# A float64 weight join with its intermediate word in PSUM, a fused state update, and a new opening list, in a one-core RWKV and mixture-of-experts kernel

## Chip, core and metric

The kernel runs on one core of a Trainium2 chip. The metric is the device time of one execution in microseconds. "Before" has three timed runs and one profiled execution.

## What is computed

The reference is a float32 RWKV attention, a bilinear feed-forward layer and a soft mixture of eight experts. Cut to what matters:

```python
for t in range(S):                       # B=4, H=8, S=768, D=48
    cur = einsum(u * k_t, v_t)
    y[:, :, t] = einsum(r_t, state + cur)
    state = w_t[..., None] * state + einsum(k_t, v_t)
x = y.transpose(0, 2, 1, 3).reshape(3072, 384)
x = ((x @ w1) * (x @ w2)) @ w3 @ w_out   # weights are float64: 384x1024, 384x1024, 1024x1024, 1024x384
P = exp(x @ w_gate - max);  8 rounds of row and column normalisation (Sinkhorn)
out = sum over e of P[:, e] * (relu(x @ e_w1[e]) @ e_w2[e])
```

The four weights of the feed-forward layer arrive as float64, two 32-bit words each. The chip makes float32 of them: the exponent and upper mantissa come from the high word, three more mantissa bits from the low word, the sign from the high word.

## The kernel before, in words

All engines run fixed instruction lists; there is no planner on the chip, and each engine and each DMA queue works strictly in the order in which the Python code issued its instructions. The order of the first 28 slices (a slice is a quarter of an attention unit of 128 tokens; there are 24 units) is written out by hand in the table `START`: each word names a step and its index. From slice 28 on (`S0`) a loop over slices issues the steps. After the 96 attention slices and the feed-forward blocks, the experts take the rest of the time with another schedule; the change does not touch that part.

Steps of the opening that matter here:

- `ld.j` (line 200) loads piece j of the float64 weights. There are 20 pieces: 4 of w_out ("o", 768 words per partition), 8 of w3 ("3", 1024 words) and 8 of w1 and w2 ("i", 768 words). Four raw buffers take turns.
- `c1.j` (lines 187 and 188) is two ScalarE operations over the whole piece: the high word scaled by 2^-112 into the result tile, and the low word turned in place into three bits.
- `c2.j` (lines 193 and 194) is two VectorE operations over the whole piece: shift the scaled word left by 3 and OR the three bits in, then OR in the sign. Every operand lies in SBUF.
- `w34.s.g` is TensorE's product of w3 and w_out, 8 rows s of 8 steps g, so that the layer's two last matrices become one; step g needs columns g*128 of the piece of w3 and part g of w_out. `ws` and `w34l` split the result into a high and a low part.
- `hi` (ScalarE) and `lo` (GpSimd) split w1 and w2 likewise. Then `pa.b.f` and `pb.b.f` (line `ab`) are the two products of token block b with column block f, `asb` copies pa out, `gs` (line 465, VectorE) multiplies, `gh` and `gl` split, and `po` multiplies by the joined matrix.
- Attention of unit n: `scanF`, `scanG`, `small`, `ks`, `rp`, `cc` on VectorE; `kx`, `rx`, `rk`, `ec` on GpSimd; `sc`, `trn`, `yt1`, `up`, `yt2` on TensorE; `Sn` (lines 375 and 376) on VectorE makes the new state in two half steps, each a product TSt of the old state with the decay, and the addition of `up` out of PSUM.

PSUM banks of the pool `ps` come from one tag `moe` with four buffers, used by w34, pa, pb, po and the logits.

Of the kernel before, what the change touches and what calls it, by code (L numbers as in the profile page):

```python
# [27 lines left out]
ks.0 L.w.2 c1.0 small.0 L.k.2 rp.0 kx.0 L.r.2 c2.0 rx.0 trn.0 c1.1 sc.0 ld.4 scanG.1 kn.0 c2.1 ks.1 ld.5 scanF.1
L.k.3 c1.2 rk.0 small.1 L.w.3 rp.1 c2.2 L.r.3 c1.3 rx.1 L.kn.2 L.rn.2 kx.1 cc.0 w34.0.0 ld.6 c2.3 ec.0 w34.0.1 c1.4
rk.1 scanG.2 ld.7 w34.0.2 w34.0.3 L.kn.3 L.rn.3 w34.0.4 c2.4 c1.5 w34.0.5 cp.0 w34.0.6 ld.8 c2.5 w34.0.7 yt1.0 ws.0  # L30
up.0 w34l.0 L.v.2 Sn.0 w34.1.0 ld.9 c1.6 w34.1.1 w34.1.2 cc.1 yt2.0 scanF.2 ec.1 w34.1.3 xraw.0 sc.1 c2.6 L.w.4 rk.2
w34.1.4 c1.7 trn.1 w34.1.5 w34.1.6 cp.1 ld.10 kn.1 w34.2.0 L.kn.4 L.rn.4 c2.7 yt1.1 w34.2.1 up.1 w34.1.7 L.v.3
small.2 ld.11 w34.3.0 c1.8 Sn.1 w34.2.2 w34.3.1 rp.2 w34.2.3 ws.1 ks.2 yt2.1 rx.2 L.r.4 c2.8 w34.2.4 L.k.4 xraw.1
w34.3.2 kx.2 w34.2.5 w34.3.3 w34l.1 w34.2.6 cc.2 ld.12 trn.2 scanF.3 ec.2 w34.3.4 kn.2 w34.2.7 scanG.3 sc.2 c1.9
rk.3 w34.3.5 small.3 w34.4.0 L.w.5 cp.2 w34.3.6 rp.3 ws.2 w34.4.1 L.kn.5 L.rn.5 c2.9 w34.3.7 rx.3 L.r.5 c1.12
w34.4.2 yt1.2 w34l.2 w34.4.3 ws.3 ks.3 up.2 ld.13 w34.4.4 c1.10 L.v.4 w34l.3 Sn.2 L.k.5 w34.5.0 kx.3 w34.4.5 w34.5.1
cc.3 yt2.2 c2.10 ec.3 w34.4.6 xraw.2 sc.3 rk.4 c1.13 w34.4.7 xd.2 trn.3 cp.3 ld.14 w34.5.2 c2.12 w34.6.0 ws.4 L.kn.6
L.rn.6 w34.5.3 c1.11 w34l.4 w34.6.1 w34.5.4 c2.13 ld.16 w34.6.2 w34.5.5 hi.0 w34.6.3 kn.3 lo.0 c2.11 w34.5.6 hi.1
w34.6.4 xh.0 yt1.3 lo.1 w34.6.5 c1.14 up.3 w34.6.6 L.v.5 scanF.4 ld.15 w34.7.0 w34.6.7 w34.7.1 ws.6 scanG.4 w34.5.7
w34l.6 w34.7.2 small.4 ws.5 L.w.6 c2.14 w34.7.3 w34l.5 w34.7.4 c1.15 w34.7.5 ks.4 ld.17 w34.7.6 xl.0 hi.2 kx.4 L.k.6  # L40
w34.7.7 ws.7 Sn.3 pa.0.0 lo.2 asb.0.0 pb.0.0 c2.15 w34l.7 c1.16 yt2.3 pa.0.1 rp.4 hi.3 c2.16 rx.4 L.r.6 xraw.3
pb.0.1 lo.3 gs.0.0 hi.4 ld.18 trn.4 cc.4 pa.0.2 gh.0.0 scanG.5 kn.4 ec.4 c1.17 sc.4 scanF.5 pb.0.2 lo.4 asb.0.1 cp.4
L.w.7 pa.0.3 small.5 c2.17 gl.0.0 c1.18 yt1.4 rk.5 up.4 gs.0.1 hi.5 ld.19 L.v.6 ks.5 pb.0.3 gh.0.1 asb.0.2 gl.0.1
c2.18 L.kn.7 L.rn.7 L.k.7 pa.0.4 lo.5 gs.0.2 hi.6 Sn.4 kx.5 pb.0.4 c1.19 rp.5 yt2.4 lo.6 asb.0.3 cc.5 L.r.7 gh.0.2
pa.0.5 gs.0.3 xraw.4 c2.19 ec.5 gh.0.3 pb.0.5 asb.0.4 gl.0.2 scanG.6 hi.7 trn.5 gl.0.3 pa.0.6 kn.5 gs.0.4 lo.7
gh.0.4 asb.0.5 gs.0.5 gl.0.4 gh.0.5 pb.0.6 asb.0.6 gl.0.5 gs.0.6 pa.0.7 rx.5 gh.0.6 gl.0.6 asb.0.7 pb.0.7 scanF.6
# [9 lines left out]
def tile_rwkv_moe_sinkhorn_moe(  # L56
# [155 lines left out]
    def c1(j):  # L212
        kind, i = CONV[j]
        if kind == "o":
            c = wo[:, 2 * i:2 * i + 2, :].rearrange("p a d -> p (a d)")
        elif kind == "3":
            c = tmp.tile([P, FF], F32, tag="w3c", bufs=3, name="w3c")
        else:
            c = tmp.tile([P, KD * FC], F32, tag="cv", bufs=2, name="cv")
        conv1(raws[j], FF, c)  # L220
        cvs[kind, i] = c

    def c2(j):
        conv2(raws.pop(j), cvs[CONV[j]])

# [995 lines left out]
```

## Time and profile before

| what | value |
|---|---|
| median of 3 runs | 1995.4 us (1994.36 to 1997.26) |
| the profiled execution, its own time | 1995.78 us |
| its span in the trace | 1993.5 us |
| TensorE busy over the span | 97% |
| VectorE, ScalarE, GpSimd busy over the span | 72%, 34%, 34% |
| mean granted clock of TensorE | 0.997 |

The span is the time from the first to the last instruction in the trace; 2.3 us of the execution's own time lie around it. A busy TensorE is not TensorE at its peak, because matmuls are pipelined and their ends are modelled; an idle TensorE, though, has a named releaser. The profile's page has one strip of 40 slices of the span for each engine: TensorE's first digits are 5 and 8 and all later ones are 9, VectorE's are 8 and 9. The stage in question is therefore the first 150 us.

### The profile page before, as it was taken

Reading aid. Unit: us, or ns where it says so; the run is one execution under the profiler, and the core shown is the slowest. Engines: PE = TensorE matmul, PEld = TensorE weight load, DVE = VectorE, ACT = ScalarE, POOL = GpSimd, SP = SyncE. Lnnn points to the kernel's source line nnn. Section 1 sums busy time; section 2 is a strip of 40 time slices with the busy share of each in tenths; the row PEclk is TensorE's granted clock in tenths of the full one; section 3 lists DMA queues with packets and bytes.
Section 4 is the critical chain, followed back from the end, with each engine's and each line's share of the span. In section 5 each row is a group of like instructions: output and inputs, shape, how many; then the busy total and the mean of one; then the engine's idle time right before and its main releaser. Section 6 shows DMA issues by size and latency. Waiting matters only on the chain.

```text
span 1993.5 us, 37983 instructions
## 1 busy us (share of the span) xinstructions
...
## 2 busy tenths in 40 slices
...
GB/s 365 178 104 102 112 145 114 132 93 179 238 187 182 188 195 170 193 177 200 172 203 187 178 201 177 203 170 201 181 184 184 188 187 185 191 193 167 179 192 121
DMA packets 90492, 353.75 MB, mean 177 GB/s; under 512 B 10384, under 2 KB 34256, under 8 KB 64592
## 3 DMA queue, kind: packets, MB, share of 16 engines
...
q14 instruction: 50, 0.41, 0.1%
...
## 4 chain that ended last, share of the span: by engine, by line
PE 87%; DVE 3%; DMA 1%; ACT 1%; issue 1%; POOL 0%; SPq 0%; DVEq 0%; ACTq 0%; POOLq 0%
PE yp L108 38%; PE zp L108 33%; PE po L108 5%; PE pa L108 4%; PE pb L108 4%; PE yt L108 1%; DMA xd<-x2s 1%; DVE ct L883 1%; DVE hl L880 1%; PE sc L108 1%; PE up L108 0%; PE trn L108 0%; DVE x2s L674 0%; PE pl L108 0%; POOL x2s L674 0%
## 5 line engine op out<-in xcount | busy, mean ns | idle before, releaser
L108 PE MATMUL zp<-xc,w1c 128*128 128x256 f32 x5760 | 841.8, 282 | 8.8 <-ACT ct L890 7.8
L108 PEld LDWEIGHTS zp<-xc,w1c 128*128 128x128 f32 x5760 | 790.3, 189 | 26.2 <-ACT ct L890 10.4
L108 PE MATMUL yp<-w2h,hh 128*128 128x384 f32 x1536 | 517.8, 337 | 0.0
L108 PE MATMUL yp<-w2h,hl 128*128 128x384 f32 x1536 | 516.9, 336 | 0.2 <-DVE hl L880 0.2
L108 PE MATMUL yp<-w2l,hh 128*128 128x384 f32 x1536 | 515.9, 336 | 0.6 <-DVE w2l L655 0.6
L875 ACT ACTIVATE hh<-ct 128x512 fp32r<-128x512 f32 x384 | 237.3, 632 | 602.0 <-DVE ct L886 323.1
L883 DVE TENSOR_TENSOR ct<-ct,zp 128x512 f32<-128x512 f32 x576 | 381.4, 683 | 58.7 <-PE zp L108 58.0
L607 POOL TENSOR_TENSOR w1c<-w1s,w1c 128x512 fp32r<-128x512 f32 (+1 forms) x120 | 132.9, 1108 | 765.5 <-PE zp L108 477.9
L108 PEld LDWEIGHTS yp<-w2h,hh 128*128 128x128 f32 x1536 | 291.6, 190 | 0.5 <-ACT w2h L654 0.2
L890 ACT ACTIVATE ct<-zp 128x512 f32<-128x512 f32 x256 | 153.1, 598 | 399.0 <-PE zp L108 399.0
L880 DVE SCALAR_TENSOR_TENSOR hl<-ct,hh 128x512 fp32r<-128x512 f32 x384 | 288.9, 766 | 1.2 <-ACT hh L875 1.2
L108 PEld LDWEIGHTS yp<-w2l,hh 128*128 128x128 f32 x1536 | 288.8, 188 | 0.8 <-DVE w2l L655 0.8
L108 PEld LDWEIGHTS yp<-w2h,hl 128*128 128x128 f32 x1536 | 288.6, 188 | 0.5 <-DVE hl L880 0.5
L1054 DVE SCALAR_TENSOR_TENSOR acc<-yp,Pm,acc 128x384 f32<-128x384 f32 x336 | 205.1, 610 | 58.0 <-PE yp L108 57.9
L886 DVE TENSOR_TENSOR ct<-ct,zp 128x512 f32<-128x512 f32 x128 | 88.1, 688 | 172.7 <-PE zp L108 172.6
L886 DVE TENSOR_TENSOR ct<-zp,ct 128x512 f32<-128x512 f32 x128 | 88.5, 692 | 137.9 <-PE zp L108 134.3
L599 POOL TENSOR_TENSOR w1s<-w1raw 128x128 f32<-128x128 f32 x240 | 127.8, 554 | 0.2
L607 POOL TENSOR_TENSOR w1c<-w1raw,w1c 128x128 fp32r<-128x128 f32 (+1 forms) x90 | 50.0, 556 | 216.5 <-ACT w1c L603 216.4
L474 POOL TENSOR_TENSOR gl<-gs,gh 128x384 fp32r<-128x384 f32 x64 | 78.8, 1232 | 121.9 <-ACT gh L470 121.8
L108 PE MATMUL pa<-xhl,w1h 128*128 128x384 f32 x384 | 104.1, 351 | 3.8 <-DVE xhl L438 3.2
L108 PE MATMUL pb<-xhl,w2h 128*128 128x384 f32 x384 | 98.5, 337 | 5.7 <-DVE gs L465 5.7
L465 DVE TENSOR_TENSOR gs<-pb,asb 128x384 f32<-128x384 f32 x64 | 35.3, 552 | 69.7 <-PE pb L108 46.9
...
## 6 DMA issues: line engine op xcount, KB each, us to landing
...
```

Source lines behind the costliest of these rows:

```text
L108: nc.tensor.matmul(o, lhsT, rhs, start=start, stop=stop, **kw)
L465: nc.vector.tensor_tensor(t, m_t.pop(("pb", blk, f)), m_t.pop(("asb", blk, f)), op=ALU.mult)
L474: nc.gpsimd.tensor_tensor(gl[:, f, :], m_t.pop(("gs", blk, f)), gh[:, f, :].bitcast(F32), op=ALU.subtract)
L599: eng.tensor_tensor(tmp_[:, many.index(r), :], at_(a), at_(b), op=ALU.add if sg == 1 else ALU.subtract)
L607: eng.tensor_tensor(lo[:, d0:d1, :], sv, hi[:, d0:d1, :].bitcast(F32), op=ALU.subtract)
L875: nc.scalar.activation(hh, src, AF.Relu)
L880: nc.vector.scalar_tensor_tensor(hl, src, 0.0, hh.bitcast(F32), op0=ALU.max, op1=ALU.subtract)
L883: nc.vector.tensor_tensor(o, a, b_, op=ALU.add)
L886: nc.vector.tensor_tensor(o, a, b_, op=ALU.subtract)
L890: nc.scalar.activation(t, src, AF.Copy)
L1054: nc.vector.scalar_tensor_tensor(dst, yp, so["Pm"][:, tt, e:e + 1], dst, op0=ALU.mult, op1=ALU.add)
```

## The change

Three things change, and nothing outside the opening and `Sn` is issued differently except for the PSUM tags.

1. The join works by halves of a piece. `lw.j` does the low word as before, over the whole piece. `ex.j.h` writes the scaled high word of half h (384 or 512 words) into a PSUM tile. `jn.j.h` does the two VectorE operations on that half: the first reads PSUM and the low word in SBUF and writes PSUM, the second reads the high word in SBUF and PSUM and writes the result in SBUF.
2. `Sn` uses one operation for each of the four head pairs, old state times decay plus `up`, in place of a product and an addition over all pairs. The tile TSt goes away.
3. `START` lists the same steps anew, with `lw`, `ex` and `jn` in place of `c1` and `c2`. The tag `moe` becomes two tags of two buffers: `mA` for w34, pa, the logits and the even po, `mB` for the PSUM halves of the join, pb and the odd po.

```diff
@@ START, of 423 words before and 483 after, first and last lines
-L.kn.0 L.kn.1 L.w.0 L.k.0 ld.0 L.r.0 L.v.0 ld.1 L.r.1 L.w.1 L.v.1 L.k.1 ld.2 L.rn.0 ldu ld.3 L.rn.1 scanG.0 scanF.0
...
-yt2.6 gs.1.0 gh.1.0 xraw.6 gl.1.0
+L.w.0 L.w.1 L.k.0 ld.0 L.r.0 ld.1 L.kn.1 L.k.1 L.r.1 scanG.0 scanF.0 ks.0 scanG.1 lw.0 ld.2 ld.3 L.kn.0 ex.0.0
...
+kx.7 L.w.9 rx.7 pa.1.0 po.0.3 asb.1.0 pb.1.0 gs.1.0 gh.1.0 gl.1.0
@@ the join
-        nc.scalar.activation(c, raw[:, :, 1].bitcast(F32), AF.Copy, scale=EXP_SHIFT)
-        nc.scalar.activation(raw[:, :, 0], raw[:, :, 0], AF.Relu, bias=lowb, scale=LOW_SCALE)
...
-        nc.vector.scalar_tensor_tensor(cu, cu, 3, lw, op0=ALU.logical_shift_left, op1=ALU.bitwise_or)
-        nc.vector.scalar_tensor_tensor(cu, hi, 0x80000000, cu, op0=ALU.bitwise_and, op1=ALU.bitwise_or)
+    def lw(j):
+        low = raws[j][:, :, 0]
+        nc.scalar.activation(low, low, AF.Relu, bias=lowb, scale=LOW_SCALE)
+
+    def ex_(j, h):
+        s_ = piece(j, h)
+        t = cvp[j, h] = ps.tile([P, s_.stop - s_.start], F32, tag="mB", bufs=2, name="cvp")
+        nc.scalar.activation(t, raws[j][:, s_, 1].bitcast(F32), AF.Copy, scale=EXP_SHIFT)
+
+    def jn(j, h):
...
+        raw, c = raws[j], cvp.pop((j, h)).bitcast(U32)
+        nc.vector.scalar_tensor_tensor(c, c, 3, raw[:, s_, 0], op0=ALU.logical_shift_left, op1=ALU.bitwise_or)
+        nc.vector.scalar_tensor_tensor(cvs[CONV[j]][:, s_].bitcast(U32), raw[:, s_, 1], 0x80000000, c,
+                                       op0=ALU.bitwise_and, op1=ALU.bitwise_or)
@@ sn_
-                ts_ = att.tile([P, NP, DP], F32, tag="TS", name="TSt")
-                nc.vector.tensor_tensor(ts_, s0, d["T12"][:, :, c].unsqueeze(2).to_broadcast([P, NP, DP]), op=ALU.mult)
-                nc.vector.tensor_tensor(sn, ts_, d["up"][c], op=ALU.add)
+                for p in range(NP):
+                    nc.vector.scalar_tensor_tensor(sn[:, p, :], s0[:, p, :], d["T12"][:, p, c:c + 1], d["up"][c][:, p, :],
+                                                   op0=ALU.mult, op1=ALU.add)
@@ tags
-            w34_acc[s] = ps.tile([P, DM], F32, tag="moe", bufs=4, name="w34ps")
+            w34_acc[s] = ps.tile([P, DM], F32, tag="mA", bufs=2, name="w34ps")
-        m_t[nm, blk, f] = pt = ps.tile([P, BLK], F32, tag="moe", bufs=4, name=nm)
+        m_t[nm, blk, f] = pt = ps.tile([P, BLK], F32, tag={"pa": "mA", "pb": "mB"}[nm], bufs=2, name=nm)
-                po_t[blk] = ps.tile([P, BLK], F32, tag="moe", bufs=4, name="po")
+                po_t[blk] = ps.tile([P, BLK], F32, tag="mAmB"[2 * (q % 2):][:2], bufs=2, name="po")
```

How the lists move, at three places. First, VectorE around the first piece of w3, on which TensorE's first w34 matmul waits (raw is the piece, cvp the PSUM half, w3c the joined w3, wo the joined w_out, Gt, Ft, Kt, Rt and cc belong to attention units 0 and 1). Before:

```order
L287 TENSOR_TENSOR Kt<-nat_k_102,Gt 128x2x8x32
L270 SCALAR_TENSOR_TENSOR Ft<-nat_w_106,d_63 128x528
L281 RECIPROCAL Mt<-Ft 128x16
L282 TENSOR_TENSOR T_211<-Ft 128x8
L291 TENSOR_TENSOR Rt<-nat_r_100,Ft 128x2x8x32
L193 SCALAR_TENSOR_TENSOR w3c<-w3c,raw 128x1024
L194 SCALAR_TENSOR_TENSOR w3c<-raw,w3c 128x1024
L308 TENSOR_REDUCE cc<-rk 128x8
```

And now:

```order
L298 TENSOR_TENSOR Rt<-nat_r_100,Ft 128x2x8x32
L227 SCALAR_TENSOR_TENSOR cvp<-cvp,raw 128x384
L228 SCALAR_TENSOR_TENSOR wo<-raw,cvp 128x384
L294 TENSOR_TENSOR Kt<-nat_k_102,Gt 128x2x8x32
L288 RECIPROCAL Mt<-Ft 128x16
L289 TENSOR_TENSOR T_215<-Ft 128x8
L227 SCALAR_TENSOR_TENSOR cvp<-cvp,raw 128x512
L228 SCALAR_TENSOR_TENSOR w3c<-raw,cvp 128x512
L227 SCALAR_TENSOR_TENSOR cvp<-cvp,raw 128x384
L228 SCALAR_TENSOR_TENSOR wo<-raw,cvp 128x384
L227 SCALAR_TENSOR_TENSOR cvp<-cvp,raw 128x512
L228 SCALAR_TENSOR_TENSOR w3c<-raw,cvp 128x512
```

Each join is now two pairs of operations on half the width, the halves of different pieces interleave, and the first half of w3c is complete with a half of wo still to come between it and the second.

Second, the DMA queue (SP) around the third and fourth piece of w_out (raw, 128x1536) and the first and second of w3 (raw, 128x2048). Before:

```order
L209 DMA raw<-in_moe_w_out_dram 128x1536
L159 DMA nat_rn_108<-in_rn_dram 128x384
L159 DMA nat_w_105<-in_w_dram 128x529
L159 DMA nat_k_101<-in_kt_dram 128x512
L159 DMA nat_r_99<-in_rt_dram 128x512
L209 DMA raw<-in_moe_w_out_dram 128x1536
L209 DMA raw<-in_moe_w_dram 128x2048
```

And now:

```order
L200 DMA raw<-in_moe_w_dram 128x2048
L200 DMA raw<-in_moe_w_out_dram 128x1536
L163 DMA nat_kn_109<-in_kn_dram 128x384
L163 DMA nat_rn_107<-in_rn_dram 128x384
L769 DMA ub<-in_u_dram 128x384
L163 DMA nat_rn_108<-in_rn_dram 128x384
L163 DMA nat_v_103<-in_v_dram 128x512
L200 DMA raw<-in_moe_w_out_dram 128x1536
```

Up to and including the first piece of w3, nat_kn of unit 0 and nat_v of units 0 and 1 are no longer in front. Up to and including the last piece of w_out, nat_v of unit 1 and nat_w, nat_k and nat_r of unit 2 are no longer in front.

Third, VectorE where block 0's pa and pb run, around the first gs (cv is a joined piece of w1 or w2). Before:

```order
L193 SCALAR_TENSOR_TENSOR cv<-cv,raw 128x768
L194 SCALAR_TENSOR_TENSOR cv<-raw,cv 128x768
L465 TENSOR_TENSOR gs<-pb,asb 128x384
L287 TENSOR_TENSOR Kt<-nat_k_102,Gt 128x2x8x32
L193 SCALAR_TENSOR_TENSOR cv<-cv,raw 128x768
L194 SCALAR_TENSOR_TENSOR cv<-raw,cv 128x768
L465 TENSOR_TENSOR gs<-pb,asb 128x384
L375 TENSOR_TENSOR TSt<-Sn,T_789 128x256
L376 TENSOR_TENSOR Sn<-TSt,up_1016 128x256
```

And now:

```order
L472 TENSOR_TENSOR gs<-pb,asb 128x384
L227 SCALAR_TENSOR_TENSOR cvp<-cvp,raw 128x384
L228 SCALAR_TENSOR_TENSOR cv<-raw,cvp 128x384
L281 SCALAR_TENSOR_TENSOR Gt<-nat_w_106,d_63 128x527
L227 SCALAR_TENSOR_TENSOR cvp<-cvp,raw 128x384
L228 SCALAR_TENSOR_TENSOR cv<-raw,cvp 128x384
L472 TENSOR_TENSOR gs<-pb,asb 128x384
L294 TENSOR_TENSOR Kt<-nat_k_102,Gt 128x2x8x32
L227 SCALAR_TENSOR_TENSOR cvp<-cvp,raw 128x384
L228 SCALAR_TENSOR_TENSOR cv<-raw,cvp 128x384
L472 TENSOR_TENSOR gs<-pb,asb 128x384
```

The halves of the join stand between one gs and the next, and pb and cvp now take turns in the same two PSUM banks: from pb.0.0 to pb.0.3 the turns fall so that each pb has the bank of the pb just before it.

## Rows read from the trace of the kernel before

**Rows 1.** The page: the chain of work that ended last, by engine.

```profile
PE 87%; DVE 3%; DMA 1%; ACT 1%; issue 1%; POOL 0%; SPq 0%; DVEq 0%; ACTq 0%; POOLq 0%
```

**Rows 2.** Stages: length; PE, PEld, DVE, ACT, POOL busy; PE clock; DMA share; GB/s.

```profile
0.00:33.70 33.70, 10.81 (x116) 6.50 (x116) 27.09 (x33) 14.44 (x16) 19.39 (x24) 1.00 0.96 362
33.70:86.80 53.10, 48.28 (x500) 27.72 (x493) 51.13 (x55) 33.40 (x48) 39.00 (x26) 1.00 0.70 248
86.80:132.20 45.40, 35.54 (x411) 31.05 (x409) 41.42 (x46) 23.97 (x41) 41.28 (x29) 0.96 0.30 102
132.20:152.40 20.20, 20.20 (x241) 18.67 (x239) 13.82 (x21) 4.95 (x12) 11.94 (x13) 1.00 0.47 139
```

**Rows 3.** TensorE's waits, 0 to 230 us: total, times, longest.

```profile
PE w34ps L108 <- DVE w3c L194: 13.8, 5, 9.9
PE trn L108 <- POOL Kt L297: 11.9, 2, 11.3
PE pb L108 <- DVE gs L465: 5.7, 3, 2.6
```

**Rows 4.** TensorE in order of time: start, length, operation, count, idle before.

```profile
23.61 6.03 PE L108 MATMUL w34ps<-wo,w3c 128*128 128x384 f32 x12 [9.86 <-DVE w3c L194]
...
31.16 1.56 PE L108 MATMUL w34ps<-wo,w3c 128*128 128x384 f32 x4 [1.52 <-DVE wo L194]
```

**Rows 5.** ScalarE in order of time, its wait for w_out's last piece.

```profile
25.24 0.94 ACT L187 ACTIVATE wo<-raw 128x768 f32<-128x768 f32 x1 [2.62 <-DMA raw<-in_moe_w_out_dram]
```

**Rows 6.** VectorE in order of time: two joins of one shape.

```profile
14.95 0.93 DVE L193 SCALAR_TENSOR_TENSOR wo<-wo,raw 128x768 uint32<-128x768 uint32 x1
...
27.70 1.74 DVE L193 SCALAR_TENSOR_TENSOR wo<-wo,raw 128x768 uint32<-128x768 uint32 x1
```

**Rows 7.** VectorE's groups, 0 to 152.4 us: busy, mean ns, idle before.

```profile
L194 DVE SCALAR_TENSOR_TENSOR w3c<-raw,w3c 128x1024 uint32<-128x1024 uint32 x8 | 13.6, 1703 | 0.3
L194 DVE SCALAR_TENSOR_TENSOR cv<-raw,cv 128x768 uint32<-128x768 uint32 x8 | 12.9, 1614 | 0.3
L193 DVE SCALAR_TENSOR_TENSOR w3c<-w3c,raw 128x1024 uint32<-128x1024 uint32 x8 | 12.0, 1503 | 0.0
L375 DVE TENSOR_TENSOR TSt<-Sn,T 128x256 f32<-128x256 f32 x12 | 11.3, 942 | 0.2
L193 DVE SCALAR_TENSOR_TENSOR cv<-cv,raw 128x768 uint32<-128x768 uint32 x8 | 10.2, 1281 | 0.0
L194 DVE SCALAR_TENSOR_TENSOR wo<-raw,wo 128x768 uint32<-128x768 uint32 x4 | 5.1, 1276 | 0.1
L376 DVE TENSOR_TENSOR Sn<-TSt,up 128x256 f32<-128x256 f32 x12 | 5.1, 422 | 1.7 <-PE w34ps L108 0.5
L465 DVE TENSOR_TENSOR gs<-pb,asb 128x384 f32<-128x384 f32 x9 | 4.9, 545 | 4.0 <-PE pb L108 3.0 <-issue 1.0
L193 DVE SCALAR_TENSOR_TENSOR wo<-wo,raw 128x768 uint32<-128x768 uint32 x4 | 4.8, 1196 | 0.1
```

**Rows 8.** The page's costliest groups: two VectorE forms that read PSUM.

```profile
L883 DVE TENSOR_TENSOR ct<-ct,zp 128x512 f32<-128x512 f32 x576 | 381.4, 683 | 58.7 <-PE zp L108 58.0
...
L1054 DVE SCALAR_TENSOR_TENSOR acc<-yp,Pm,acc 128x384 f32<-128x384 f32 x336 | 205.1, 610 | 58.0 <-PE yp L108 57.9
```

**Rows 9.** Duration of the state update's addition, all instances: min/median/max.

```profile
L376 DVE TENSOR_TENSOR Sn<-TSt,up x12: 421/422/422, 35.6 to 149.8; 128x256 f32<-128x256 f32 x12
```

**Rows 10.** ScalarE's groups, 0 to 152.4 us, the scaled high word.

```profile
L187 ACT ACTIVATE w3c<-raw 128x1024 f32<-128x1024 f32 x8 | 9.2, 1151 | 8.6 <-PE w34ps L108 4.9 <-DMA raw<-in_moe_w_dram 3.7
L187 ACT ACTIVATE cv<-raw 128x768 f32<-128x768 f32 x8 | 7.3, 918 | 5.9 <-POOL w1l L237 3.4 <-POOL w2l L237 1.4 <-DMA raw<-in_moe_w_dram 1.1
```

**Rows 11.** Busy time in one stretch inside the third stage, columns as in Rows 2.

```profile
112.00:116.00 4.00, 3.41 (x22) 2.65 (x25) 3.76 (x5) 2.82 (x5) 4.00 (x4) 0.60 0.11 42
```

**Rows 12.** VectorE in order of time, two short operations.

```profile
44.62 0.25 DVE L281 RECIPROCAL Mt<-Ft 128x16 f32<-128x16 f32 x1
44.78 0.10 DVE L282 TENSOR_TENSOR T<-Ft 128x8 f32<-128x8 f32 x1
```

More of the change, by code (lines that the diff above doesn't have):

```diff
@@ L26 @@
 START = """
-L.kn.0 L.kn.1 L.w.0 L.k.0 ld.0 L.r.0 L.v.0 ld.1 L.r.1 L.w.1 L.v.1 L.k.1 ld.2 L.rn.0 ldu ld.3 L.rn.1 scanG.0 scanF.0
[L28 to L46, printed above, removed]
@@ new lines @@
+rp.1 lw.2 ld.4 L.r.2 jn.1.1 ks.1 ex.2.0 ld.5 L.v.1 small.1 lw.3 L.w.2 jn.2.0 kx.1 ex.3.0 rk.0 jn.3.0 ex.2.1 w34.0.0
+jn.2.1 ex.3.1 w34.0.1 rx.1 cc.0 lw.4 ld.6 w34.0.2 L.kn.2 jn.3.1 ec.0 L.k.2 ex.4.0 w34.0.3 jn.4.0 ex.4.1 ld.7 rk.1
+w34.0.4 L.rn.2 kn.0 L.k.3 cp.0 w34.0.5 ex.5.0 jn.4.1 yt1.0 up.0 ex.5.1 scanF.2 w34.0.6 lw.5 w34.0.7 Sn.0 jn.5.0
+yt2.0 lw.6 ld.8 L.r.3 L.rn.3 small.2 w34.1.0 L.w.3 cc.1 xraw.0 L.kn.3 sc.1 rp.2 L.v.2 jn.5.1 ex.6.0 rx.2 trn.1
+w34.1.1 ws.0 ec.1 w34.1.2 jn.6.0 lw.7 w34.1.3 rk.2 cp.1 w34.1.4 ex.6.1 kn.1 w34.2.0 jn.6.1 ex.7.0 w34.1.5 w34l.0
```

64 lines of the change are left out of this document (38 added, 26 removed).

## The prediction, made before the changed kernel was run

> **What bounds the kernel now.** The chain of work that ended last is read first: 87% of it is TensorE [rows 1]. So a gain can only come where TensorE stands idle. The busy times by stage come next, cut at the ends of TensorE's work: unit 0's up (33.7 us), the last w34 (86.8), the last pb of block 0 (132.2), and the opening's end (152.4) [rows 2]. From 132.2 us on TensorE is busy throughout. Before that it is idle for 33.70 - 10.81 = 22.9 us, for 53.10 - 48.28 = 4.8 us, and for 45.40 - 35.54 = 9.9 us. VectorE is busy 27.09, 51.13 and 41.42 us in these stages, in the second 96% of it, so it sets the pace there; the waits say the same, since the largest that is not the start itself is for VectorE's join of w3, and the next for gs, which stands behind joins in VectorE's list [rows 3]. The first stage has a second limit: the DMA engines are full (0.96), and ScalarE waits for the last piece of w_out until 25.24 us [rows 2, 5].
>
> Then the joins themselves. The same operation on 768 words took 0.93 us at 15 us, where GpSimd stood idle, and 1.74 us at 28 us, where it worked [rows 6]; on average it took 1.20 to 1.61 us [rows 7]. The addition that ends Sn, in the same stretch and with GpSimd as busy, took 421 to 422 ns every time [rows 9]: it has one operand in PSUM and one in SBUF. gs, of the same kind, has a mean of 545 ns for 384 elements [rows 7]. So an operation with two operands in SBUF is stretched, one with an operand in PSUM is not. That decides this change, because both operations of a half join, and the fused Sn, have one of their two tensors in PSUM.
>
> **The joins.** Now they cost 13.6 + 12.9 + 12.0 + 10.2 + 5.1 + 4.8 = 58.6 us of VectorE [rows 7]. After: 12 pieces of 768 words in four operations of 384, and 8 of 1024 in four of 512. For those I take the rows with one tensor in PSUM, 0.55 us for 384 (gs) [rows 7] and 0.68 us for 512 [rows 8]: 48 x 0.55 + 32 x 0.68 = 48.2 us, 10.4 less. No row shows VectorE writing PSUM, so I bound it: from below by the undisturbed SBUF form, 0.93 us for 768 [rows 6], less 384 elements at the slope of the two rows above, (683 - 545)/128 = 1.08 ns, gives 0.52 us, and 0.65 for 512: 45.8 us; from above by the dearest such form, 0.61 us for 384 [rows 8], and 0.75 for 512: 53.3 us. The nearest are the two I took, as they have one tensor in each memory.
>
> **Sn.** Twelve half steps cost 11.3 + 5.1 = 16.4 us [rows 7]. After, each is four operations of 64 elements. The form with a decay per partition took 610 ns for 384 [rows 8]; 320 elements less is 0.26 us, 48 of them 12.7 us. Short operations that do not need each other overlap: one of 0.25 us was followed after 0.16 us [rows 12], 0.09 less. The other end is the elements alone, 64 x 1.08 ns, 3.3 us in all. I take 0.26 - 0.09 = 0.17 us, or 8.2 us: 8.2 less (3.7 to 13). After slice 28 this hides behind TensorE, which is busy there; without that cover it would be a gain, not a cost.
>
> Together VectorE loses 18.6 of its 119.6 busy microseconds before 132.2 us, and GpSimd is no longer held up by the joins.
>
> **ScalarE.** The scaled high word cost 1.15 us for 1024 and 0.92 us for 768 [rows 10], 0.91 ns per element and 0.22 us fixed. Halves cost that 0.22 us once more, 20 x 0.22 = 4.4 us, unless writing PSUM has another price. ScalarE is busy 72 of 132 us, so I cost it at nothing; if ScalarE's list gets behind, the join is late by 0.6 us per half.
>
> **First stage.** Two things move w34's start. The first piece of w3 has 640 KB less in front of it in the queue (kn of unit 0, v of units 0 and 1), 1.8 us at 362 GB/s [rows 2]; and the first w34 needs one half joined, 2 x 0.68, not the whole, 3.2 us [rows 7]. So w34 can start 3.6 us earlier than 23.61 [rows 4], at 20 us. But its last two steps need the last piece of w_out, which has 1032 KB less in front (v of unit 1; w, k and r of unit 2): 2.9 us at the same rate, so ScalarE starts on it at 22.3 us in place of 25.24 [rows 5]. Then come the low word (about as long as the high one, 0.9), a half word 0.6 and four half operations 2.2: joined at 26.0, where w34's last two steps now start at 31.16 [rows 4]. Other work on VectorE may stand between, so I take 4.5 us. The ends are 5 and, with the loads no earlier, 2.
>
> **Second stage.** 4.8 us of idle time, all of it small waits for joins and what stands behind them [rows 2, 3]. VectorE's seven pieces of w3 here fall from 22.4 to 19.0 us and each releases TensorE after its first half; I keep 2 us of waiting, for second halves: 2.8 us, from 0 to 4.8.
>
> **Third stage.** 9.9 us idle, and 1.6 us lost where the granted clock was 0.60 over 4 us [rows 11], a mixture of the two levels of 1.2 and 2.4 GHz; I count on none of that coming back. The stage holds five pieces of w1 and w2, 2.9 us each now and 2.2 after, and four half steps of Sn, 1.36 and 0.68: VectorE's 41.4 us become 35.2, as much as TensorE's 35.5 [rows 2], and it comes in with a lead. I keep 2.7 us of waits: 7.2 us, from 2 to 11.5, which is everything and the clock.
>
> **Sum.** 4.5 + 2.8 + 7.2 = 14.5 us off the profiled execution's 1995.8, gives 1981.3; the median of the runs is 0.4 below that execution, and I state 1981.5. Ends: 5 + 4.8 + 11.5 = 21.3 gives 1974.5; 2 + 0 + 2 = 4 gives 1991.8. The tags cost nothing after slice 28: pa and pb alternate, so each has the bank of two before, as it did with four.
>
> **Rivals.** *The banks decide.* pb.0.1, pb.0.2 and pb.0.3 wait for the gs before them, because halves of the join take the other bank of mB. Between the first two gs stand two half joins (2.2 us) and a scan, while TensorE has one pa and one pb. If VectorE arrives there without a lead, the 5.7 us of waits for gs [rows 3] stay and grow by what else was won: the third stage gives 0, and the sum is 7.3, 1988.5. For it: VectorE is as full in that stage (91%). Against: its load before that stage is lighter by 12 us. Chance 0.2.
>
> *The loads decide.* The DMA engines are full to 33.7 us. If joins then wait for pieces, the first stage gives 2, the second nothing and the third 2, at 1991.8. For: 0.96. Against: 0.70 in the second stage. Chance 0.1.
>
> *The cut costs more than it frees, slower.* The place is VectorE before 132 us. There are 40 more join operations and 24 more for Sn, each with its fixed part; on rows 0.55 - 0.41 = 0.14 us each. If a write into PSUM is dear, or the stretching is not taken away but moves to the scans and Kt and Rt, VectorE has no relief. The change does not do then what it says. It decides from the point where 48x + 32(x + 0.14) exceeds 58.6 + 8.2 us, that is x above 0.78 us for 384 words, against the 0.52 to 0.61 in rows. At 0.84 us VectorE has 5 us more work, all of it TensorE's waits: 2001. Chance 0.07. The Trainium skill speaks for this rival: "VectorE: DVE Perf Modes", section "The TRN2 errata — SBUF-src ops pay a fixed extra latency per instruction", gives a fixed cost per instruction of 58 cycles from SBUF and 120 from PSUM, and advises tiles of at least 512 elements. By it four halves of 384 are an estimated 2.1 us against 1.72 for the whole piece, 0.38 us more for each of 20 pieces, 7.6 us, so about 2003. The trace agrees with the fixed part, but the same whole pieces took 2.5 to 2.9 us here, which that table does not hold.
>
> **How the numbers follow.** The forecast case has 0.6, with the range 1974.5 to 1986; the rivals have 0.2, 0.1 and 0.07; 0.03 is left. 1975 to 1992 takes in the first two and most of the loads' case. A measurement of this kernel can tell 0.2%, 4 us, from no change: faster is below 1991.4. That is the forecast, the banks and half the loads: 0.86; same 0.07; slower 0.07.
>
> **What would show it.** Right: joins of 384 words at 0.55 us with almost no spread, w34's first matmul near 20 us, the end of the opening (pa and pb of block 1) near 138 us in place of 152.4, waits for w3c and gs of a few microseconds in all, GpSimd's operations shorter. Wrong: halves over 0.7 us or as scattered as now; scans much longer; TensorE's waits for gs above 6 us; a gain that is there at 138 us and is lost later to a new wait.

## The result, and the profile after

The changed kernel takes 1976.7 us in the median of four runs (1975.24 to 1980.37), the kernel before, run beside it, 1996.3. The ratio is 0.9906, with a 95% interval of 0.9892 to 0.9921: 19.7 us or 0.9% faster. The forecast was 1981.5, with a range of 1975 to 1992. The profiled execution is the slowest of the four, 1980.37 us with a span of 1978.7, so the two profiled executions lie only 15.4 us apart.

The chain of work that ended last, by engine, against [rows 1]:

```profile
PE 90%; DVE 4%; DMA 3%; ACT 1%; issue 1%; POOL 1%; SPq 0%; DVEq 0%; ACTq 0%; POOLq 0%
```

The stages with the columns of [rows 2], cut at the same points of TensorE's work: unit 0's up, the last w34, the first po (132.2 before), and pb of block 1 (the end of the list, 152.4 before):

```profile
0.00:26.60 26.60, 9.47 (x113) 6.03 (x114) 20.94 (x41) 12.46 (x19) 11.71 (x24) 1.00 0.92 355
26.60:78.10 51.50, 48.69 (x498) 28.99 (x499) 46.86 (x95) 38.37 (x62) 26.29 (x28) 1.00 0.82 299
78.10:116.40 38.30, 35.34 (x540) 32.44 (x539) 33.68 (x69) 24.12 (x48) 37.02 (x34) 1.00 0.46 148
116.40:132.93 16.53, 16.53 (x112) 16.21 (x107) 6.78 (x13) 4.24 (x11) 5.35 (x7) 1.00 0.43 137
```

The opening ends at 132.9 us in place of 152.4, 19.5 us earlier; nothing is gained behind it. Two pieces of work change their stage. The last four matmuls of w34's row 0 (the second line of [rows 4]) ran ahead of unit 0's up before and run behind it now, which puts them into the second stage. Unit 0's up before, and now:

```profile
33.17 0.65 PE L108 MATMUL up<-nat_v,kn 64*64 64x64 f32 x32
```

```profile
25.92 0.64 PE L112 MATMUL up<-nat_v,kn 64*64 64x64 f32 x30
26.49 1.56 PE L112 MATMUL w34ps<-wo,w3c 128*128 128x384 f32 x4
```

Both are done at 33.82 us before and at 28.05 now, 5.8 us earlier; that leaves 2.9 for the second stage. And some attention work of unit 6 now comes before the first po, so the last two stages have to be read together: 65.6 us before, 54.8 now.

VectorE's joins and Sn, to 136.2 us (busy, mean ns, idle before), against [rows 7]:

```profile
L227 DVE SCALAR_TENSOR_TENSOR cvp<-cvp,raw 128x384 uint32<-128x384 uint32 x24 | 13.4, 556 | 2.6 <-ACT cvp L214 2.5
L227 DVE SCALAR_TENSOR_TENSOR cvp<-cvp,raw 128x512 uint32<-128x512 uint32 x16 | 11.1, 693 | 1.5 <-ACT cvp L214 1.4
L228 DVE SCALAR_TENSOR_TENSOR w3c<-raw,cvp 128x512 uint32<-128x512 uint32 x16 | 11.0, 688 | 0.8
L382 DVE SCALAR_TENSOR_TENSOR Sn<-Sn,T,up 128x64 f32<-128x64 f32 x48 | 9.8, 274 | 0.5 <-PE up L112 0.2
L228 DVE SCALAR_TENSOR_TENSOR cv<-raw,cvp 128x384 uint32<-128x384 uint32 x16 | 8.9, 554 | 0.8
L228 DVE SCALAR_TENSOR_TENSOR wo<-raw,cvp 128x384 uint32<-128x384 uint32 x8 | 4.4, 554 | 0.3
```

The joins come to 13.4 + 11.1 + 11.0 + 8.9 + 4.4 = 48.8 us, where they were 58.6. How little they scatter is seen in minimum, median and maximum of all instances:

```profile
L228 DVE SCALAR_TENSOR_TENSOR w3c<-raw,cvp x16: 686/688/696, 18.0 to 64.2; 128x512 uint32<-128x512 uint32 x16
L228 DVE SCALAR_TENSOR_TENSOR cv<-raw,cvp x16: 553/555/556, 54.9 to 101.5; 128x384 uint32<-128x384 uint32 x16
```

TensorE's waits up to 230 us, against [rows 3] (total, times, longest):

```profile
PE sc L112 <- POOL Rt L310: 10.5, 1, 10.5
PE w34ps L112 <- DVE w3c L228: 7.7, 2, 6.0
PE trn L112 <- POOL Rt L310: 1.1, 1, 1.1
...
PE pb L112 <- DVE cv L228: 0.8, 1, 0.8
```

Waits for w3c fell from 13.8 to 7.7 us, and those of pb for gs, 5.7 us, are no longer in the list. TensorE in order of time around its first w34, against [rows 4]:

```profile
18.73 5.82 PE L112 MATMUL w34ps<-wo,w3c 128*128 128x384 f32 x12 [6.05 <-DVE w3c L228]
```

and ScalarE at the last piece of w_out, against [rows 5]:

```profile
22.07 1.02 ACT L209 ACTIVATE raw<-raw,lowb 128x768 uint32<-128x768 uint32 x1 [1.77 <-DMA raw<-in_moe_w_out_dram]
```

### The profile page after: what moved, and what is told of

Read it like the earlier page. It is cut to its first block, busy times and chain, and to the rows that moved or that the text cites. A ratio compares the mean times of both kernels' runs of the same rounds, so it can differ in the third digit from the quotient of the medians.

```text
span 1978.7 us, 38130 instructions
## 1 busy us (share of the span) xinstructions
PE 1934.8 (98%) x15499; PEld 1871.5 (95%) x15499; DVE 1401.1 (71%) x2427; ACT 685.9 (35%) x1320; POOL 637.0 (32%) x859
## 4 chain that ended last, share of the span: by engine, by line
PE 90%; DVE 4%; DMA 3%; ACT 1%; issue 1%; POOL 1%; SPq 0%; DVEq 0%; ACTq 0%; POOLq 0%
PE yp L112 38%; PE zp L112 33%; PE pa L112 5%; PE pb L112 5%; PE po L112 5%; PE yt L112 1%; DMA xd<-x2s 1%; DVE ct L890 1%; DMA raw<-in_moe_w_dram 1%; DVE hl L887 1%; PE trn L112 1%; PE sc L112 1%; PE up L112 1%; PE w34ps L112 0%; DVE cvp L227 0%
## 5 line engine op out<-in xcount | busy, mean ns | idle before, releaser
L890 DVE TENSOR_TENSOR ct<-ct,zp 128x512 f32<-128x512 f32 x576 | 381.5, 683 | 58.6 <-PE zp L112 58.0
L481 POOL TENSOR_TENSOR gl<-gs,gh 128x384 fp32r<-128x384 f32 x64 | 74.8, 1170 | 126.4 <-ACT gh L477 126.4
L472 DVE TENSOR_TENSOR gs<-pb,asb 128x384 f32<-128x384 f32 x64 | 35.4, 553 | 80.7 <-PE pb L112 58.6
```

The lines of the kernel that those rows point to most:

```text
L472: nc.vector.tensor_tensor(t, m_t.pop(("pb", blk, f)), m_t.pop(("asb", blk, f)), op=ALU.mult)
L481: nc.gpsimd.tensor_tensor(gl[:, f, :], m_t.pop(("gs", blk, f)), gh[:, f, :].bitcast(F32), op=ALU.subtract)
L890: nc.vector.tensor_tensor(o, a, b_, op=ALU.add)
```

## The experiments

Two theories stood at the start. Theory 1: VectorE sets the pace of the opening, and what frees it is that an operation with a tensor in PSUM is not held up by GpSimd. Theory 2: the new list and the earlier loads do it, and the place of the word hardly matters. As a mark of the opening that all kernels share, the text uses the start of the transposes of unit 7 (trn): 157.1 us before, 137.6 in the changed kernel, and 138.4 in its repetition.

**The changed kernel again.** No edit.

> The changed kernel again, for a firmer size of the gain. In the profiled executions the opening ended 16.2 us earlier, while the medians of four runs lie 19.7 us apart. If the whole gain is in the opening, the ratio here is near 0.992 (16 us); if something after the opening is faster too, it is near 0.990 (20 us).

Measured: 1976.9 us, ratio 0.9906 (0.9891 to 0.992), kernel before 1996.8. The gain is firm; its profiled span is 1973.9 us. The 16.2 us of the expectation set 152.4 against a later point of the list, 136.2; at the same point of the work the opening ends 19.5 us earlier, so the whole gain lies in the opening. The execution shown above lost some 5 us behind the mark against this one (1978.7 - 137.6 against 1973.9 - 138.4), which says nothing of the change. Below, "the changed kernel" is 1976.9.

**The word in SBUF.** New list, halves and new state stay. Only the scaled word lies in SBUF: in its own half of the result tile (`made` allocates that tile earlier), or in one extra tile for the first halves of pieces 8 to 11.

```diff
-        t = cvp[j, h] = ps.tile([P, s_.stop - s_.start], F32, tag="mB", bufs=2, name="cvp")
+        if 8 <= j < 12 and h == 0:
+            t = tmp.tile([P, FF // 2], F32, tag="cvp", bufs=1, name="cvp")
+        else:
+            t = made(j)[:, s_]
```

> The changed kernel with the half word of the join in SBUF in place of PSUM, all else as changed. Theory 1, the operand in PSUM keeps GpSimd from stretching the joins: operations of 384 words go from 0.55 us back to 0.6 to 0.9 us and scatter, VectorE gets 8 to 13 us more before the opening ends, and 7 to 12 us of the gain are lost. Theory 2, the new order and the halves make the gain: the joins may be longer, but no more than 3 us are lost.

Measured: 1997.7 us, ratio 1.0006 (0.9997 to 1.0015). The whole gain is gone, which is Theory 1's direction at twice its size. It is lost in the opening: the mark is at 159.3 us, 20.9 later than in the repetition. The earlier allocation does not explain it, as VectorE waited 1.2 us for the scaled word here and 3.3 in the repetition. The second operations on the pieces of w1 and w2, which took 553 to 556 ns with the word in PSUM (minimum, median, maximum):

```profile
L236 DVE SCALAR_TENSOR_TENSOR cv<-raw,cv x16: 557/854/1255, 63.8 to 123.6; 128x384 uint32<-128x384 uint32 x16
```

VectorE in this kernel, in order of time:

```profile
20.33 1.23 DVE L236 SCALAR_TENSOR_TENSOR wo<-raw,wo 128x384 uint32<-128x384 uint32 x1
21.49 1.48 DVE L235 SCALAR_TENSOR_TENSOR w3c<-w3c,raw 128x512 uint32<-128x512 uint32 x1
23.00 0.99 DVE L236 SCALAR_TENSOR_TENSOR w3c<-raw,w3c 128x512 uint32<-128x512 uint32 x1
23.91 0.54 DVE L323 TENSOR_REDUCE cc<-rk 128x8 f32<-128x384 f32 x1
24.37 0.54 DVE L235 SCALAR_TENSOR_TENSOR wo<-wo,raw 128x384 uint32<-128x384 uint32 x1
```

GpSimd in the same stretch:

```profile
19.84 1.30 POOL L280 TENSOR_TENSOR rk<-nat_rn,nat_kn 128x384 f32<-128x384 f32 x1
21.23 1.19 POOL L281 TENSOR_TENSOR rk<-rk,ub 128x384 f32<-128x384 f32 x1
22.38 1.06 POOL L318 TENSOR_TENSOR Rt<-Rt,Mt 128x256 f32<-128x256 f32 x1
23.40 1.07 POOL L318 TENSOR_TENSOR Rt<-Rt,Ft 128x256 f32<-128x256 f32 x1
24.53 1.29 POOL L327 TENSOR_TENSOR ec<-eye,cc 128x512 f32<-128x512 f32 x1
```

The same operations of GpSimd in the changed kernel, with the word in PSUM:

```profile
18.66 1.00 POOL L272 TENSOR_TENSOR rk<-nat_rn,nat_kn 128x384 f32<-128x384 f32 x1
19.75 1.00 POOL L273 TENSOR_TENSOR rk<-rk,ub 128x384 f32<-128x384 f32 x1
20.71 0.61 POOL L310 TENSOR_TENSOR Rt<-Rt,Mt 128x256 f32<-128x256 f32 x1
21.28 0.62 POOL L310 TENSOR_TENSOR Rt<-Rt,Ft 128x256 f32<-128x256 f32 x1
```

With the word in SBUF, each join ends about half a microsecond behind the end of one GpSimd operation (20.33 + 1.23 = 21.56 after 19.84 + 1.30 = 21.14, then 22.97 after 22.42, 23.99 after 23.44): the engines take turns. At 24.37 the join took 0.54 us, most of it beside the next GpSimd operation, which started at 24.53, took 1.29 us where it took 1.04 in the changed kernel, and so was the one to wait. Sorted by whether a GpSimd operation ran for a tenth of its time or more, the joins of this kernel are: 384 words, 18 without at a mean of 0.555 us and 30 with at 1.11; 512 words, 7 at 0.684 and 25 at 1.15. In the changed kernel, 384 words: 14 without at 0.554, 34 with at 0.557. The Trainium skill, "SBUF — State Buffer", section "🔬 SBUF: two separate sides", describes an exclusive lock on a port pair: a VectorE operation with two SBUF inputs and a GpSimd operation that reads SBUF block each other for the whole instruction. The rows agree (0.555 us without a GpSimd operation, 1.11 with one), and they show that an operand in PSUM avoids it (0.554 and 0.557).

Why twice the size: the time lost is about the same for each operation, not for each word. Kernel before: 0.49 us for 768 words (0.95 without GpSimd, 1.44 with; only three operations ran without), 0.40 for 1024 (a single one ran without). Here: 0.56 for 384, 0.46 for 512. Halves have twice as many operations, and 55 of 80 meet GpSimd where 36 of 40 did before; each operation has a part that does not shrink besides. So the joins take 76.6 us, the sum of their groups, against 48.8 with PSUM and 58.6 before: 27.8 us more of VectorE go with 20.8 us of time. GpSimd was busy longer as well, 96.9 us up to the mark against 83.3 in the repetition (114.9 before), and no run separates what its delay costs from what VectorE's does.

**The old state update in the changed kernel, and the new state update alone in the kernel before.**

```diff
-                for p in range(NP):
-                    nc.vector.scalar_tensor_tensor(sn[:, p, :], s0[:, p, :], d["T12"][:, p, c:c + 1], d["up"][c][:, p, :],
...
+                ts_ = att.tile([P, NP, DP], F32, tag="TS", name="TSt")
+                nc.vector.tensor_tensor(ts_, s0, d["T12"][:, :, c].unsqueeze(2).to_broadcast([P, NP, DP]), op=ALU.mult)
+                nc.vector.tensor_tensor(sn, ts_, d["up"][c], op=ALU.add)
```

> The changed kernel with the old state update (product TSt, then addition). The twelve half steps of the opening cost VectorE 16.4 us in the kernel before and cost 9.8 now. Theory 1, VectorE sets the pace of the opening still: 3 to 6 us are lost. Theory 2, TensorE sets it since the change: under 2 us are lost, and nothing after slice 28.

> The kernel before with the new state update alone. VectorE is full there, so if its load alone counts, 6 us less of it give 3 to 5 us; if the order of the list and the loads hold TensorE, under 2 us.

Measured: 1981.8 us, ratio 0.9923 (0.9911 to 0.9935), and 1992.3 us, ratio 0.9981 (0.9973 to 0.999). By medians the state update is worth 4.9 us on top of the rest and 4.5 us alone (and 4.0 with the word in SBUF, in the table below). The mark in the traces moved less, from 138.4 to 140.0 and from 157.1 to 155.7. Its direction is shown, its size is between 1.5 and 5 us.

**The list and the halves alone.** The word in SBUF and the old state, both edits above.

> The changed kernel's list and halves alone: the word in SBUF (the result tile itself, and for the first halves of w3 pieces 8 to 11 one extra tile), and the state scaled and added by the old two operations. If the effects of the parts add up: the kernel with the word in SBUF and the new state took 1997.7, and the old state added about 4 to 5 us to the changed kernel, so 2001 to 2004, slower than the kernel before. If the list and the earlier loads are a gain of their own that the stretched joins only hid in part: at or below 1997.

Measured: 2001.7 us, ratio 1.0029 (1.0018 to 1.0041). The list, the earlier loads and the halves by themselves are a loss of 5 us. The parts add up, as the first of the two forecasts had it (2001 to 2004). So Theory 2 falls as it was put. How much of the loss is the list and how much the cut into halves was not separated. The kernels side by side:

| kernel | us | ratio |
|---|---|---|
| before | 1996.8 | 1 |
| before, new state | 1992.3 | 0.9981 |
| list and halves, word in SBUF, old state | 2001.7 | 1.0029 |
| list and halves, word in SBUF, new state | 1997.7 | 1.0006 |
| list and halves, word in PSUM, old state | 1981.8 | 0.9923 |
| all (the change) | 1976.9 | 0.9906 |

PSUM is worth 19.9 us with the old state and 20.8 with the new one. PSUM with the old list was not tried: there w34 keeps up to three PSUM tiles open at once, and four is all that the pool has for them, pa, pb and po. Nor was PSUM with whole pieces, so what the cut into halves costs or gives in the change itself is not shown.

**Quarters.** Each half's two joins are cut once more, the word stays in PSUM: VectorE gets work that GpSimd cannot stretch.

```diff
+        m = (s_.stop - s_.start) // 2
+        for a in (0, m):
+            ca, sa = c[:, a:a + m], slice(s_.start + a, s_.start + a + m)
...
```

> The changed kernel with each half's two joins cut once more (quarters of a piece, word still in PSUM): 80 more VectorE operations in the opening, no other engine changed. From the changed kernel's rows, 0.555 us for 384 elements and 0.690 us for 512, one operation has a part of about 0.15 us that does not shrink, so VectorE gets 80 x 0.15 = 12 us more, with nothing of it from the port it shares with GpSimd. Theory 1 (VectorE still sets the pace of the opening after the change): 6 to 11 us slower than the changed kernel, 1983 to 1988. Theory 2 (TensorE sets the pace now, since it waits for only 7 us behind its first w34 product): at most 3 us slower.

Measured: 1985.3 us, ratio 0.9947 (0.9935 to 0.996). VectorE's joins in this kernel:

```profile
L230 DVE SCALAR_TENSOR_TENSOR cvp<-cvp,raw 128x192 uint32<-128x192 uint32 x48 | 17.3, 360 | 2.0 <-ACT cvp L214 1.2
L230 DVE SCALAR_TENSOR_TENSOR cvp<-cvp,raw 128x256 uint32<-128x256 uint32 x32 | 13.7, 428 | 0.5
L231 DVE SCALAR_TENSOR_TENSOR w3c<-raw,cvp 128x256 uint32<-128x256 uint32 x32 | 13.5, 421 | 1.3
L231 DVE SCALAR_TENSOR_TENSOR cv<-raw,cvp 128x192 uint32<-128x192 uint32 x32 | 11.3, 354 | 1.4
L231 DVE SCALAR_TENSOR_TENSOR wo<-raw,cvp 128x192 uint32<-128x192 uint32 x16 | 5.7, 354 | 0.5
```

They come to 61.5 us, 12.7 more, and the kernel is 8.4 us slower (the mark at 148.1 us, 9.7 later than in the repetition). This is Theory 1: even after the change, TensorE follows VectorE through the opening, though it shows few waits for it. From 192 to 384 words an operation grows by 554 - 354 = 200 ns, so 154 ns of it do not shrink; the undisturbed joins in SBUF, 0.95 us for 768 and 0.555 for 384, give 0.16 in the same way. The table in the Trainium skill, "VectorE: DVE Perf Modes", section "The TRN2 errata — SBUF-src ops pay a fixed extra latency per instruction", has more than twice as many fixed cycles for PSUM as for SBUF, and the text under it puts the measured fixed part of an operation on SBUF near 150 cycles instead (an estimated 156 ns at the table's 0.96 GHz); the rows show 154 and 160 ns, no difference between the two memories. The exchange rate is 8.4/12.7 = 0.66, and with the word in SBUF it was 20.8/27.8 = 0.75.

**The old order of loads.** The first 17 loads go out as in the kernel before, the rest of the list stays.

```diff
-L.w.0 L.w.1 L.k.0 ld.0 L.r.0 ld.1 L.kn.1 L.k.1 L.r.1 scanG.0 scanF.0 ks.0 scanG.1 lw.0 ld.2 ld.3 L.kn.0 ex.0.0
+L.kn.0 L.kn.1 L.w.0 L.k.0 ld.0 L.r.0 L.v.0 ld.1 L.r.1 L.w.1 L.v.1 L.k.1 ld.2 L.rn.0 ldu ld.3 L.rn.1 scanG.0 scanF.0
```

> The changed kernel with the first 17 loads issued in the order of the kernel before (both kn first, w.1 in tenth place, w3's first piece in thirteenth); everything else as changed. Theory 1 (the first stage was shortened by joins alone): the first scan starts near 6.3 us instead of 3.65, but the first w34 product moves by less than 1 us and the time by less than 1 us. Theory 2 (the part of the first stage's gain that the forecast missed came from the loads' order): the first w34 product comes 1.5 to 3 us later than 18.73 us and the time is 1.5 to 3.5 us longer than the changed kernel's.

Measured: 1980.7 us, ratio 0.9922 (0.9908 to 0.9935). By medians it is 3.8 us slower than the changed kernel, though the two intervals overlap a little; the mark, at 141.7 us, is 3.3 later than in the repetition. VectorE's first scan in this kernel, in order of time, and TensorE's first w34:

```profile
6.69 1.26 DVE L281 TENSOR_TENSOR_SCAN Gt<-nat_w,d 128x527 f32<-128x527 f32 x1 [4.86 <-DMA nat_w<-in_w_dram]
```

```profile
24.32 5.97 PE L112 MATMUL w34ps<-wo,w3c 128*128 128x384 f32 x9 [4.52 <-DVE w3c L228]
```

The first scan starts at 6.69 us where the changed kernel has 3.65, and the first w34 comes 5.6 us later, later than in the kernel before (23.61). Part of this is the list itself, which wants the scan of w.1 early: VectorE waited 9.1 us for the two nat_w in all, 1.8 in the changed kernel. Theory 2 of this run holds in its direction, though the first w34 moved further than its 1.5 to 3 us: with the word in PSUM, a late start of VectorE is paid at the end.

**An early table load, without and with another order of the list.** Both aim at TensorE's first 18.7 us.

```diff
     lt = const.tile([GP * UB, P], F32, name="lt")
+    warm = const.tile([P, 1], F32, name="warm")
+    nc.scalar.activation(warm, lowb, AF.Relu, bias=lowb, scale=LOW_SCALE)
```

```diff
-L.w.0 L.w.1 L.k.0 ld.0 L.r.0 ld.1 L.kn.1 L.k.1 L.r.1 scanG.0 scanF.0 ks.0 scanG.1 lw.0 ld.2 ld.3 L.kn.0 ex.0.0
...
+L.w.0 L.k.0 ld.0 L.r.0 ld.2 L.w.1 ld.1 ld.3 L.kn.0 L.rn.0 ldu scanG.0 scanF.0 ks.0 lw.0 ex.0.0 small.0 ex.0.1 rp.0 kx.0
...
```

> The changed kernel with one ScalarE operation on a single column put at the start, so that the table load of 1.28 us, which stood between the landing of the first piece (7.75 us) and its low words, is done before. If VectorE's stream sets the pace from the first join on: the first join starts 1 us earlier than 10.46 us, VectorE's wait of 1.08 us ahead of it goes, the first w34 product comes 0.5 to 1 us earlier and the time falls by 0.5 to 1 us, hardly more than can be measured. If loads set the first stage: the first w34 product stays within 0.3 us of 18.73 us and the time is unchanged.

> As the kernel with the early table load, and the first 70 entries of the list put in another order: w3's first piece is loaded ahead of w.1 and of w_out's second piece and joined first, the scans and products of unit 1 come behind it. If the wait for the first joined half of w3 (6.05 us in the changed kernel) is a real part of the path: first w34 product at 14 to 16 us instead of 18.73, and 1 to 4 us faster than the changed kernel. If VectorE's total work sets the time whatever its order: TensorE waits later for what it gained, for w3c or for unit 1, and the time stays within 1 us of the kernel with the table load alone, or is longer.

Measured: 1986.1 us, ratio 0.9947 (0.9935 to 0.9959), and 1987.8 us, ratio 0.9955 (0.9941 to 0.9969). The first fits neither forecast. Its first w34 is at 18.97 us, where the loads' theory had it: the first piece landed at 8.62 us in this execution, not at 7.75, so the low words began only 0.4 us earlier. The mark stands where it was (138.5), but the time is 9.2 us longer; that is taken up below. In the second, TensorE in stretches of 4 us (columns as in [rows 2]):

```profile
18.00:22.00 4.00, 2.20 (x5) 0.64 (x3) 3.90 (x8) 1.91 (x3) 2.24 (x2) 1.00 1.05 384
22.00:26.00 4.00, 2.80 (x4) 1.00 (x4) 3.78 (x9) 2.43 (x4) 2.74 (x5) 0.52 1.03 415
26.00:30.00 4.00, 2.96 (x66) 2.38 (x66) 2.98 (x5) 1.79 (x3) 2.91 (x3) 0.50 1.03 416
30.00:34.00 4.00, 4.00 (x24) 1.74 (x24) 3.86 (x13) 2.46 (x4) 0.00 (x0) 0.70 1.02 405
```

The first w34 did come early, at 15.44 us. But single pieces of w_out now came late (waits of 3.0 us for wo), and behind a few matmuls with gaps the granted clock stood at 0.50, the lower level of 1.2 GHz, and was back at 1.00 only from 33 us on. The mark came at 140.8, 2.3 later than with the table load alone, and the median is 1.7 us longer. So the forecast by VectorE's total work fits: TensorE waited later for what it had gained. How much of the 2.3 us is the lower clock is not separated.

**What the table load cost: the operation or its tile.** Two kernels separate them: the same early operation, written into a tile that exists, and the tile alone, set by VectorE.

```diff
+    nc.scalar.activation(L[:, 0, 0:1], lowb, AF.Relu, bias=lowb, scale=LOW_SCALE)
```

```diff
+    warm = const.tile([P, 1], F32, name="warm")
+    nc.vector.memset(warm, 0.0)
```

> The kernel with the early table load took 1986.1, 9 us more than the changed kernel, and its opening ended as early: the time went in the products behind it, 9007 matmuls from 650 to 1950 us where the changed kernel has 9062. Here the table is loaded as early, but the one-column result goes into a tile that exists already, so that no tile moves. If the extra tile of 4 bytes per partition (it moves what stands behind it in SBUF) was the cause: 1975 to 1978, with 9050 or more matmuls from 650 to 1950 us. If the early ScalarE operation is the cause: 1984 to 1988.

> The changed kernel with a tile of one column (4 bytes per partition) more among the constants, set once by a VectorE operation of 0.06 us, and no early table load. If the extra tile is the cause: 1984 to 1988, with about 9007 matmuls from 650 to 1950 us. If the early ScalarE operation is the cause: 1976 to 1978.

Measured: 1975.1 us, ratio 0.9894 (0.9881 to 0.9908), and 1984.3 us, ratio 0.9944 (0.993 to 0.9957). The tile is the cause. One stretch behind the opening (length, PE, PEld, DVE, ACT, POOL busy, clock, DMA share, GB/s), first with the operation and no new tile, then with the tile alone:

```profile
650.00:1950.00 1300.00, 1300.00 (x9063) 1286.60 (x9062) 913.64 (x1448) 417.79 (x774) 315.03 (x504) 1.00 0.53 186
```

```profile
650.00:1950.00 1300.00, 1299.85 (x9003) 1288.19 (x9003) 911.70 (x1441) 418.20 (x772) 315.67 (x504) 1.00 0.53 186
```

TensorE is busy all the time and at full clock in both, but with the extra tile it gets 60 of 9063 matmuls less done, 0.66%, or 8.6 us of these 1300. In the same stretch every kernel of this text without that tile has 9060 to 9064, the kernel before and the two with the word in SBUF (with an extra tile of their own, in another pool) among them; so the comparisons above are free of this effect. With the early operation and no tile the first w34 came at 17.83 us in this execution; its 1975.1 cannot be told from the changed kernel's 1976.9.

**One VectorE operation of units 1 to 4 moved to GpSimd**, on top of the early operation without a tile.

```diff
-        nc.vector.tensor_tensor(diag(t), nat["k", n % 2].rearrange("p (a b s) -> p b a s", b=2, s=32), gv, op=ALU.mult)
+        (nc.gpsimd if 1 <= n <= 4 else nc.vector).tensor_tensor(diag(t), nat["k", n % 2].rearrange("p (a b s) -> p b a s", b=2, s=32), gv, op=ALU.mult)
```

> The changed kernel with the early table load into a tile that exists, and the product of k by its decays (one VectorE operation of 0.69 us) made by GpSimd for units 1 to 4. VectorE loses 4 x 0.69 = 2.8 us of the opening and up to 1 us of waiting ahead of the first join. If VectorE's stream still sets the pace (0.8 us of the end for each of its us, by the kernel in quarters): 1.5 to 3 us faster than the changed kernel, 1974 to 1975.5. If GpSimd's longer turn delays the scores or stretches VectorE's scans: no gain, or slower.

Measured: 1975.2 us, ratio 0.9896 (0.9882 to 0.9909): no more than the early operation alone. VectorE lost less than the 2.8 us: Kt costs it 3.0 us in place of 5.8 up to the mark, but the scan of Ft, Rt and xhl together cost it 1.1 more. GpSimd needs 1.2 us for what VectorE did in 0.69, and TensorE has a new wait behind it:

```profile
L295 POOL TENSOR_TENSOR Kt<-nat_k,Gt 128x512 f32<-128x512 f32 x4 | 4.8, 1197 | 5.4 <-PE trn L112 3.1 <-issue 2.2
```

```profile
PE trn L112 <- POOL w34l L258: 1.8, 1, 1.8
```

No run beats the changed kernel by more than can be measured.

## Why the prediction was right

*The bound.* Right as to VectorE. TensorE follows VectorE through the opening; the quarters show it by adding work to VectorE alone (the word in SBUF lengthens GpSimd's operations too). Too narrow as to TensorE: the forecast looked for gain only where TensorE stands idle, and 4.8 of the 19.5 us came out of its busy time.

*The joins.* Right, and closely: 48.8 us against 48.2, 0.55 us for 384 words and 0.69 for 512, and the instances of the second operation lie within 10 ns of each other. The mechanism that decided the forecast, that a tensor in PSUM takes a join out of GpSimd's way, is shown by the kernel with the word in SBUF. What the forecast did not see is how much hung on it: without PSUM the same halves take 76.6 us, 18 more than the whole pieces did. GpSimd is relieved as well, as the forecast's signs had it, 83.4 us busy up to the mark in place of 114.9; what that is worth by itself is not shown.

*Sn.* Right in direction. Four operations take 0.85 us together in the trace, each starting 0.19 us behind the one before, where 0.17 was taken. VectorE's 16.4 us became 9.8, 6.6 less and not 8.2.

*ScalarE at nothing.* Not refuted. VectorE waited 4.0 us in all for the scaled word; no wait of TensorE names it, but TensorE shows few waits for VectorE either while it follows it, so some of this may have been paid.

*First stage.* The term that was too small: 4.5 us forecast, 5.8 measured for the same work (the 7.1 of the stage's length hold 1.3 us of w34 that moved behind the cut). Its times came out nearly as worked out: ScalarE at the last piece of w_out at 22.07 us (22.3), the first w34 at 18.73 (20; VectorE's first scan, which the forecast did not count, starts at 3.65 us in place of 6.32), and the last steps of w34's row 0 start at 26.49 in place of 31.16, 4.7 us earlier. What it left out is that the list now lets TensorE do unit 0's yt and up, 1.1 us, while it waits for those steps. The forecast put 2.5 us of this stage on the earlier loads (4.5 against 2 without them); the kernel with the old order of loads came 3.3 us later at the mark. One term was misread without a consequence for the sum: the loads of kn of unit 0 and v of units 0 and 1 are 192 + 256 + 256 = 704 KB, not 640, so the first piece of w3 could come 2.0 us earlier, not 1.8.

*Second stage.* 2.8 forecast, 2.9 measured for the same work (3.4, and 0.5 less for the third stage, if the cut is put at the end of the last w34 in both, 87.28 and 78.07). Idle time fell from 4.8 to 2.8 us, so the 2 us of waits that were kept came out at 2.8; the other 0.9 us came from TensorE's busy time.

*Third stage.* 7.2 forecast; with the po work, which has to be counted with it, 10.8 measured (65.6 to 54.8). The waits kept, 2.7 us, are 3.0 in the trace (38.30 - 35.34). The rest is that TensorE's busy time fell as well, from 35.54 + 20.20 to 35.34 + 16.53 us, 3.9 less. 1.6 of this is the granted clock, which the forecast said it would not count on and which is now 1.00 in the whole stage. Where the other 2.3 us went is not worked out. A likely part is the record itself: a run of w34 matmuls shows more time for each where it is short (two alone 0.91 us, a run of 20 took 6.72, 0.34 each), so a stream with gaps looks busier than the work in it.

*The sum.* The idle time that went is 22.9 + 4.8 + 9.9 - (17.1 + 2.8 + 3.0) = 14.7 us, and the terms of the forecast were 14.5. That these are so close is partly luck: by stages the idle time fell by 5.8, 2.0 and 6.9 us where 4.5, 2.8 and 7.2 were forecast, and the differences cancel. The 4.8 us that TensorE's busy time lost on top were not in the sum; that is nearly the whole of what it missed, 19.5 against 14.5, and why the opening ended at 132.9 us and not near 138. The stated 1981.5 also does not follow from the sum as it is told: 1981.3 less 0.4 is 1980.9.

*The rivals.* The banks did not decide: waits for gs are 0.6 us. The loads did not decide against the change; their order helped it. The loss from the cut is real where PSUM is left out, but by GpSimd's hold on each operation, and not by a dear write to PSUM (0.556 us for 384 words, as dear as a write to SBUF); that list and halves alone took 2001.7, beside the rival's 2001, is chance.
